# Making the second table's angles on ScalarE, turning the tables early, and putting y0 between the token halves

## The chip, the cores and the metric

The kernel runs on one core of one Trainium2 chip. The metric is the device time of one execution in microseconds (us), taken as the median of several runs; lower is better. In the notes, PE is the matmul engine, PEld its weight loads, DVE is VectorE, ACT is ScalarE, POOL is GpSimd and SP the engine that issues most stores.

## The reference

The input `x` is 8 sequences of 3008 tokens of 256 features. The reference takes the real part of a two-dimensional Fourier transform, and then a mixer over tokens and over channels:

```python
X = np.fft.fft(np.fft.fft(x, axis=1), axis=2).real          # x: 8 x 3008 x 256
h = np.maximum(X.transpose(0, 2, 1) @ w_tok1, 0.0) @ w_tok2  # 3008 -> 256 -> 3008
u = X + h.transpose(0, 2, 1)
out = u + np.maximum(u @ w_ch1, 0.0) @ w_ch2                 # 256 -> 1536 -> 256
```

The channel products at the end are most of the arithmetic. The kernel never forms the Fourier transform along the tokens in full: it splits the length 3008 into 64 times 47 and carries the second split's tables (`tp` and `tq`, cosine and sine of 2 pi k r / 3008) into `w_tok1`, which gives the "carried" weights `hp` and `hq`.

## The kernel before

Before any product can run, the tables have to be made on the chip: an angle is computed, brought into one period (`reduced`: multiply and add 2^23, take it off again, add), and put through ScalarE's Sin. For `tp` VectorE does the angle arithmetic, for `tq` GpSimd does it.

```python
def reduced(m, period, nrow, width, eng=nc.vector):
    v = gen.tile([P, width], FP32, tag="gv", bufs=2, name="gv")[0:nrow, :]
    eng.tensor_scalar(out=v, in0=m, scalar1=1.0 / period, scalar2=TWO23, op0=AT.mult, op1=AT.add)
    eng.tensor_scalar(out=v, in0=v, scalar1=-TWO23, scalar2=-float(period), op0=AT.add, op1=AT.mult)
    r = gen.tile([P, width], FP32, tag="gr", bufs=2, name="gr")[0:nrow, :]
    eng.tensor_tensor(out=r, in0=v, in1=m, op=AT.add)
    return r

def angles3(off, eng):
    m3 = gen.tile([P, 768], FP32, tag="m3", bufs=2, name="m3")
    ts(m3[:], kb[:], reff[:], AT.mult, off[:], AT.add, eng=eng)
    return reduced(m3[:], S, P, 768, eng)

table3(tp, angles3(offp, nc.vector))
# ... small tables on VectorE (ident, anti, md, t1n, t1b) ...
r3q = angles3(offq, pl)                # pl is GpSimd
```

Each batch then has a front: VectorE (batch 0) or GpSimd (later batches) folds the input (`fold`: xd, xp, eo), PE makes stage 1 (`pz`, copied to `z`) and stage 2 (`pw`, copied to `w`), and in batch 0 the carried weights (`ph`) in rounds between the `pw` products. The tail of the front is the token mixer: two halves of `w_tok1` products (`pt`), with `sq`, `uv` and `uu` made of them by ScalarE and VectorE; a small product `px` with a permutation that fills one column of `w`; thirds of `y` (`third`); and then the `w_tok2` products (`pu`).

```python
for th in range(2):
    c = slice(th * P, (th + 1) * P)
    pt = ps_f("pt1")                   # ps_f: a PSUM tile of 512 f32, three buffers in turn
    for o, n, f, hw in ((0, 130, 0, hp), (130, 127, 132, hq)):
        for g in range(NG):
            nc.tensor.matmul(pt[:, o:o + n], lhsT=hw[:, g, c], rhs=w[:, g, f:f + n], ...)
    if th == 0:
        px = ps_f("px")                # its own tile
        nc.tensor.matmul(px[:, 0:NG], lhsT=perm[:], rhs=w[:, :, 130], start=True, stop=True)
        nc.scalar.activation(out=w[:, :, 131], in_=px[:, 0:NG], func=AFT.Copy)
    sq = ...; nc.scalar.activation(out=sq[:], in_=pt[:, 130:257], func=AFT.Copy)
    # ... uv by VectorE from pt and sq, uu by ScalarE from uv ...
    yield
# ...
for c in range(NCH):
    if c < 3:
        third(c)
        yield
    # ... pu = w_tok2 products from uu; ut = pu + y ...
```

Every `yield` gives PE's turn back to the channel products of the previous batch, so one "step" of `w_ch1` products (`pc`, 6 products of 512 columns, about 1.3 us) and one of `w_ch2` products (`po`) stand between two pieces. At the front of batch 0 there is no previous batch, and short dummy products (`filler`) fill some gaps.

## Time and profile before

The kernel before takes 635.52 us in the rounds shared with the changed kernel. Its profiled execution has a span of 634.1 us. First the head of its profile page (span, busy time of each engine, and the clock granted to PE in 40 slices, in tenths):

```profile
span 634.1 us, 11971 instructions
PE 610.8 (96%) x4806; PEld 422.4 (67%) x4806; DVE 356.7 (56%) x807; ACT 315.8 (50%) x677; POOL 248.7 (39%) x238
PEclk9999999999999999999999999999999999999999
```

PE is busy 96% of the span, so only PE's idle time can be won. Where that idle time lies is shown by busy time in windows (columns: the window, its length, then busy us and instruction count of PE, PEld, DVE, ACT and POOL, PE's granted clock, DMA share, GB/s):

```profile
0.00:20.44 20.44, 6.47 (x47) 5.01 (x48) 18.37 (x55) 10.60 (x17) 18.52 (x30) 1.00 0.99 148
20.44:28.48 8.04, 6.51 (x66) 5.11 (x67) 6.50 (x15) 7.38 (x12) 6.99 (x16) 1.00 1.09 216
28.48:35.80 7.32, 7.07 (x73) 6.22 (x74) 5.43 (x16) 6.37 (x20) 1.93 (x2) 1.00 1.27 206
35.80:43.23 7.43, 6.12 (x87) 4.96 (x85) 3.63 (x12) 3.22 (x11) 0.00 (x0) 1.00 1.05 208
43.23:634.10 590.87, 584.65 (x4538) 401.12 (x4535) 322.80 (x712) 288.23 (x618) 221.30 (x191) 1.00 0.44 82
```

The windows are cut at events: first stage-1 product 20.44, first `pw` 28.48, first token product 35.80, first `w_ch1` product 43.23. From 43.23 us on PE is nearly always busy; this stretch is called the loop below. All of PE's other idle time is in the front, 0 to 43.23 us. The clock column reads 1.00 also where the trace holds no clock record, which is before 23.65 us here, so an early 1.00 says nothing: 16 fillers took 1.91 us from 21.22 us here.

What holds the front is VectorE. Here is VectorE's timeline just before and in the fold (start, us, engine, line, operation, out<-in, shapes, count):

```profile
13.00 0.81 DVE L87 TENSOR_SCALAR t1n<-cs,mask_149 94x48 f16<-94x48 f32 x1
13.72 0.23 DVE L87 TENSOR_SCALAR t1n<-cs,xicol 94x48 f16<-94x48 f32 x1
13.87 0.84 DVE L89 TENSOR_SCALAR t1b<-cs,xicol 94x24 f16<-94x24 f32 x1
14.71 0.68 DVE L393 TENSOR_TENSOR xd<-xp,xm 94x1024 f16<-94x1024 f16 x1
15.42 2.18 DVE L394 TENSOR_TENSOR xp<-xp,xm 94x1024 f16<-94x1024 f16 x1
...
24.75 0.48 DVE L402 TENSOR_TENSOR eo<-xd 94x635 f16<-94x635 f16 x1
```

and GpSimd's timeline beside it:

```profile
13.85 0.84 POOL L228 TENSOR_SCALAR gv<-gv 128x768 f32<-128x768 f32 x1
14.77 2.28 POOL L231 TENSOR_TENSOR gr<-gv,m_198 128x768 f32<-128x768 f32 x1
```

The same table operation takes 0.81 us once and 0.23 us the next time, and the fold's first xp add takes 2.18 us where all its like take about 0.7. The 0.84 us and the 2.18 us end within 0.6 us of the end of a GpSimd operation. The fold ends at 25.23 us.

### The profile page before, as it was taken

The page shows a single profiled execution, that of the slowest core. Times are in us where ns is not written, and L with a number is a line of the kernel's source. Part 1 is how long each engine was busy: PE and PEld are TensorE (multiplying, and loading weights), DVE is VectorE, ACT ScalarE, POOL GpSimd, SP SyncE. Part 2 cuts the span into 40 slices and gives each one's busy share as a digit, 9 for nine tenths or more (in the row PEclk, how much of TensorE's full clock was granted, in tenths as well). Part 3 has the DMA queues.
Part 4 walks back from the last instruction along what each step waited for, and adds up shares of the span by engine and source line. Part 5 has one row for each costly group of instructions (what it writes and reads, how often), then busy time and mean ns, then how long its engine had stood idle before and what let it go on. Part 6 is the DMA issues. An engine that isn't in the chain of part 4 may idle for free.

```text
span 634.1 us, 11971 instructions
## 1 busy us (share of the span) xinstructions
PE 610.8 (96%) x4806; PEld 422.4 (67%) x4806; DVE 356.7 (56%) x807; ACT 315.8 (50%) x677; POOL 248.7 (39%) x238
## 2 busy tenths in 40 slices
PE   2789999999999999999999999999999999999996
PEld 1665667667666776667667676666766676666664
DVE  8866545675764556545664547645565456644442
ACT  6667465654436553374435554365444644334441
POOL 8739789497030960259220790049300000000000
PEclk9999999999999999999999999999999999999999
DMA  8992662916613459152962249433222422323432
GB/s 133 210 173 84 127 126 42 161 46 119 130 34 67 101 101 103 45 98 51 141 95 62 57 85 119 83 75 84 51 51 63 88 52 51 83 67 83 60 84 66
DMA packets 86583, 56.28 MB, mean 89 GB/s; under 512 B 54864, under 2 KB 83472, under 8 KB 85776
## 3 DMA queue, kind: packets, MB, share of 16 engines
q1 hardware_dynamic: 78048, 37.84, 31.3%
q0 software_dynamic: 8256, 17.49, 16.6%
q8 instruction: 37, 0.61, 0.4%
q10 hardware_dynamic: 224, 0.20, 0.1%
q14 instruction: 18, 0.15, 0.1%
HBM read 34.98 MB, written 24.64 MB: 94 GB/s over the span
## 4 chain that ended last, share of the span: by engine, by line
PE 92%; issue 1%; ACT 1%; DVE 0%; DVEq 0%; ACTq 0%
PE po L566 39%; PE pc L545 38%; PE pu L512 6%; PE pz L415 1%; PE py L485 1%; PE pq L485 1%; PE pw L443 1%; PE pw L442 1%; PE pz L431 0%; PE pz L425 0%; ACT c_714 L548 0%; DVE osb L583 0%; PE pt_5989 L457 0%; PE pt_4067 L457 0%; PE pt_3176 L457 0%
## 5 line engine op out<-in xcount | busy, mean ns | idle before, releaser
L545 PE MATMUL pc<-ut,wc1p 128*128 128x512 f16 x576 | 140.2, 379 | 0.4 <-DVE ut L520 0.2
L545 PE MATMUL pc<-ut,wc1m 128*128 128x512 f16 (+1 forms) x576 | 134.9, 370 | 0.0
L583 DVE TENSOR_TENSOR osb<-po,rt 128x258 f32<-128x258 f32 (+4 forms) x246 | 75.2, 356 | 50.2 <-PE po L566 44.1
L545 PEld LDWEIGHTS <-wc1m 128*128 128x128 f16 x576 | 54.8, 98 | 53.8
L545 PEld LDWEIGHTS <-wc1p 128*128 128x128 f16 x576 | 52.9, 98 | 49.1 <-issue 2.1
L520 DVE TENSOR_TENSOR ut<-pu,yt 128x512 f16<-128x512 f32 (+1 forms) x96 | 64.4, 672 | 19.7 <-PE pu L512 19.7
L393 POOL TENSOR_TENSOR xd<-xp,xm 94x1024 f16<-94x1024 f16 x28 | 59.3, 2119 | 19.3 <-DMA xm<-in_x_dram,ix_76 19.3
L394 POOL TENSOR_TENSOR xp<-xp,xm 94x1024 f16<-94x1024 f16 x28 | 59.4, 2121 | 2.2
L398 POOL TENSOR_TENSOR eo<-xp 94x512 f16<-94x512 f16 (+1 forms) x28 | 34.0, 1213 | 59.1 <-PE pz L431 57.9
L276 ACT ACTIVATE z<-pz 128x480 f16<-128x480 f32 (+1 forms) x61 | 39.7, 668 | 27.1 <-PE pz L415 22.0
L512 PE MATMUL pu<-w2p,uu 128*128 128x512 f16 (+1 forms) x168 | 50.0, 379 | 0.0
L276 ACT ACTIVATE w<-pw 128x127 f16<-128x127 f32 x96 | 25.8, 280 | 47.0 <-PE pw L443 47.0
L490 DVE TENSOR_TENSOR yt<-py,qs 128x512 f16<-128x512 f32 x48 | 30.9, 686 | 30.9 <-PE pc L545 15.6
L445 DVE SCALAR_TENSOR_TENSOR w<-alt,pw 128x131 f16<-128x131 f16 x96 | 32.8, 351 | 18.6 <-ACT w L276 18.6
L603 POOL COPY ch<-c_7328 128x768 f16<-128x768 f16 x1 | 0.8, 825 | 84.5 <-DVE c_7328 L87 84.5
L402 POOL TENSOR_TENSOR eo<-xd 94x508 f16<-94x508 f16 (+1 forms) x28 | 33.7, 1204 | 0.0
L512 PEld LDWEIGHTS <-uu 128*128 128x128 f16 x192 | 18.7, 98 | 12.5 <-ACT sq L466 1.0
L488 ACT ACTIVATE qs<-pq 128x512 f32<-128x512 f32 x24 | 14.4, 601 | 19.3 <-PE pq L485 9.3
L442 PE MATMUL pw<-td_190,z 128*128 128x128 f16 x96 | 20.4, 220 | 0.9 <-DVE z L274 0.7
L415 PEld LDWEIGHTS <-eo 94*128 94x128 f16 x240 | 15.8, 101 | 7.9 <-DVE eo L400 2.5
L605 POOL COPY c_7994<-ch 128x768 f16<-128x768 f16 x1 | 0.8, 828 | 51.2 <-PE po L566 51.2
L415 PE MATMUL pz<-t1n,eo 94*128 94x96 f16 x240 | 18.6, 211 | 2.1 <-DVE eo L400 2.1
(429 smaller groups left out, 1169.4 us busy)
## 6 DMA issues: line engine op xcount, KB each, us to landing
out_dram<-osb SPq DMA_DIRECT2D x83, 256.0 KB, 3.6
xp<-in_x_dram POOLq DMA_DIRECT2D x16, 272.0 KB
out_dram<-osb SPq DMA_DIRECT2D x11, 192.0 KB, 3.0
xp<-in_x_dram POOLq DMA_DIRECT2D x16, 127.5 KB
rt<-ut SPq DMA_TRANSPOSE x96, 3.7
w2s<-in_moe_w_tok_dram POOLq DMA_DIRECT2D x1, 1504.0 KB
w1p<-in_moe_w_tok_dram POOLq DMA_DIRECT2D x2, 384.0 KB
wc_148<-in_moe_w_ch_dram POOLq DMA_DIRECT2D x1, 768.0 KB
```

What stands on the lines that cost most here:

```text
L276: nc.scalar.activation(out=out_, in_=in_, func=AFT.Copy)
L393: eng.tensor_tensor(out=xd[:, t, :], in0=xp[:, t, :], in1=rv, op=AT.subtract)
L394: eng.tensor_tensor(out=xp[:, t, :], in0=xp[:, t, :], in1=rv, op=AT.add)
L398: eng.tensor_tensor(out=eo[:, t, 1:129], in0=xp[:, t, 1:129], in1=xp[:, t, 255:127:-1], op=AT.add)
L402: eng.tensor_tensor(out=eo[:, t, 129:256], in0=xd[:, t, 1:128], in1=xd[:, t, 255:128:-1], op=AT.subtract)
L415: nc.tensor.matmul(pz[:, 96 * k:96 * k + 96], lhsT=eo[:, t0 + k, c], rhs=t1n[:].rearrange("p a b k -> p (a b k)"), start=True, stop=True)
L445: nc.vector.scalar_tensor_tensor(out=w[:, g, 0:131], in0=alt[:], scalar=pw[:, 131:132], in1=pw[:, 0:131], op0=AT.mult, op1=AT.add)
L512: nc.tensor.matmul(pu[:, 0:n], lhsT=uu[:, th, int(minus), h, :], rhs=w2_cols(b, c)[:, th], start=(th == 0), stop=(th == 1))
L520: nc.vector.tensor_tensor(out=ut[:, h, f0:f0 + n].rearrange("p (a b) -> p a b", b=64), in0=pu[:, 0:n].rearrange("p (b a) -> p a b", b=64), ...
L545: nc.tensor.matmul(pc[:, 0:n], lhsT=wc[:, h, ct * P:(ct + 1) * P], rhs=ut[:, h, f0:f0 + n], start=(h == 0), stop=(h == 1))
L566: nc.tensor.matmul(po[0:n, o:o + D], lhsT=c1[:, ct, ks * P:ks * P + n], rhs=wc2[:, ct, :], start=(ct == 0), stop=(ct == NCT - 1))
L583: nc.vector.tensor_tensor(out=osb[r, ks_, j], in0=src[r, k0:k1, j], in1=rt[r, ks_, p], op=AT.add)
```

## The change

The intent was to free the front of batch 0. The angles of `tq` leave GpSimd, where they held VectorE (0.81 us for 0.23 and 2.18 us for about 0.7, above): three ScalarE passes with Identity and one VectorE operation make them. The second table is turned before stage 1. Two of the twelve `w_tok1` (carried) products go before the end of the fold, and the rounds shrink from seven to six. The `px` product moves ahead of the token products, into a free corner of the products' own PSUM tile, which saves a tile and a late copy. `y`'s first third (y0) goes between the two token halves. The core of the diff:

```diff
-    table3(tp, angles3(offp, nc.vector))
+    for o, i, scale, bias in ((mq, kb, reff[:], offq), (vq, mq, 1.0 / S, up),
+                              (vq, vq, 1.0, down)):
+        nc.scalar.activation(out=o[:], in_=i[:], func=AFT.Identity, scale=scale, bias=bias[:])
+    ts(mp[:], kb[:], reff[:], AT.mult, offp[:], AT.add)
+    table3(tp, reduced(mp[:], S, P, 768))
...
-    r3q = angles3(offq, pl)
+    nc.vector.scalar_tensor_tensor(out=vq[:], in0=vq[:], scalar=-float(S), in1=mq[:],
+                                   op0=AT.mult, op1=AT.add)
...
-        for th in range(2):
+        def tok1(th):
             pt = ps_f("pt1")
+            if th == 0:
+                nc.tensor.matmul(pt[:, 260:260 + NG], lhsT=perm[:], rhs=w[:, :, 130], ...)
+                nc.scalar.activation(out=w[:, :, 131], in_=pt[:, 260:260 + NG], func=AFT.Copy)
             for o, n, f, hw in (...):          # the token products into pt
-            if th == 0:
-                px = ps_f("px")                # px product and its copy, cut
...
+        tok1(0)
+        yield
+        third(0)
+        yield
+        tok1(1)
+        yield
...
     turn(tp, tts_p, 8)
-    turn_rows(tts_p, 1.0, 24)
+    table3(tq, vq)
+    turn_rows(tts_p, 1.0, 0)
     take(fold(0, [nc.vector] * 4), 4)
+    turn(tq, tts_q, 4)
     own = front(0)
     take(own, 2)
-    filler(16)
-    table3(tq, r3q)                            # ... turn(tq), turn_rows between stage-1 parts, cut
+    turn_rows(tts_q, -1.0, 16)
     take(own, 2)
-    for g2 in range(NG // 2 + 1):
-        if g2 < NG // 2:
-            take(own, 2)
-            carried(tts_p, hp, g2, 0)
-        if g2 > 0:
-            carried(tts_q, hq, g2 - 1, g2 % 3 > 0)
+    for g2 in range(2):
+        carried(tts_p, hp, g2, 0)
+    take(own, 4)
+    for g2 in range(NG // 2):
+        take(own, 2)
+        if g2 < 4:
+            carried(tts_p, hp, g2 + 2, 0)
+        carried(tts_q, hq, g2, g2 < 4)
```

More of the change, by code (lines that the diff above doesn't have):

```diff
@@ L293 @@
     sin(cs[0:KR, :], r1, PI2 / 47)
-    def angles3(off, eng):
-        m3 = gen.tile([P, 768], FP32, tag="m3", bufs=2, name="m3")
-        ts(m3[:], kb[:], reff[:], AT.mult, off[:], AT.add, eng=eng)
-        return reduced(m3[:], S, P, 768, eng)
-    table3(tp, angles3(offp, nc.vector))
+    up, down = pvec("up"), pvec("down")
+    nc.vector.memset(up[:], TWO23)
+    nc.vector.memset(down[:], -TWO23)
+    mp, mq, vq = (gen.tile([P, 768], FP32, tag=n, name=n) for n in ("mp", "mq", "vq"))
+    for o, i, scale, bias in ((mq, kb, reff[:], offq), (vq, mq, 1.0 / S, up),
+                              (vq, vq, 1.0, down)):
+        nc.scalar.activation(out=o[:], in_=i[:], func=AFT.Identity, scale=scale,
+                             bias=bias[:])
+    ts(mp[:], kb[:], reff[:], AT.mult, offp[:], AT.add)
+    table3(tp, reduced(mp[:], S, P, 768))
     ident = const.tile([P, P], FP16, tag="ident")
@@ L451, in front @@
         uu = perb.tile([P, 2, 2, 2, P], FP16, tag="uu", name="uu", bufs=2)
-        for th in range(2):
+        def tok1(th):
             c = slice(th * P, (th + 1) * P)
             pt = ps_f("pt1")
+            if th == 0:
+                nc.tensor.matmul(pt[:, 260:260 + NG], lhsT=perm[:], rhs=w[:, :, 130],
+                                 start=True, stop=True)
+                nc.scalar.activation(out=w[:, :, 131], in_=pt[:, 260:260 + NG],
+                                     func=AFT.Copy)
             for o, n, f, hw in ((0, 130, 0, hp), (130, 127, 132, hq)):
@@ L459, in front @@
                                      start=(g == 0), stop=(g == NG - 1))
-            if th == 0:
-                px = ps_f("px")
-                nc.tensor.matmul(px[:, 0:NG], lhsT=perm[:], rhs=w[:, :, 130],
-                                 start=True, stop=True)
-                nc.scalar.activation(out=w[:, :, 131], in_=px[:, 0:NG], func=AFT.Copy)
             sq = perb.tile([P, 127], FP32, tag="sq", name="sq", bufs=2)
@@ L476, in front @@
                 nc.scalar.activation(out=o, in_=i, func=AFT.Relu)
-            yield
         yt = perb.tile([P, 2, HALF], FP16, tag="yt", name="yt")
@@ L502, in front @@
         for c in range(NCH):
-            if c < 3:
+            if c in (1, 2):
                 third(c)
@@ L612 @@
     turn(tp, tts_p, 8)
-    turn_rows(tts_p, 1.0, 24)
+    table3(tq, vq)
+    turn_rows(tts_p, 1.0, 0)
     take(fold(0, [nc.vector] * 4), 4)
+    turn(tq, tts_q, 4)
     own = front(0)
     take(own, 2)
-    filler(16)
-    table3(tq, r3q)
+    turn_rows(tts_q, -1.0, 16)
     take(own, 2)
-    turn(tq, tts_q, 0)
-    take(own, 2)
-    turn_rows(tts_q, -1.0, 0)
-    take(own, 2)
-    for g2 in range(NG // 2 + 1):
-        if g2 < NG // 2:
-            take(own, 2)
-            carried(tts_p, hp, g2, 0)
-        if g2 > 0:
-            carried(tts_q, hq, g2 - 1, g2 % 3 > 0)
+    for g2 in range(2):
[6 more added lines that the diff above has]
+        carried(tts_q, hq, g2, g2 < 4)
     take(own, 5)
```

## The prediction

> **What bounds the kernel now.** The page shows PE busy 610.8 of 634.1 us (96%); the chain of waits is 92% PE. Busy time by windows: from the first w_ch1 product (43.23 us) to the end PE is busy 584.65 of 590.87 us, over 4 us of the rest being the last output write. Only the front, 0 to 43.23 us, can give anything; PE idles 17 us there. 2% (12.7 us) is out of reach.
>
> **The front's chain (timelines of the engines).** VectorE tables to 14.7, VectorE fold 14.71 to 25.23, stage-1 z copies to 28.4, pw/ph rounds 28.48 to 35.8 (about 1.13 us each), token tail 35.8 to 43.23.
>
> **What the change does.**
> 1. GpSimd loses four 768-wide operations (11.69 to 17.05 us). Meanwhile VectorE was held: small table operations took 0.81 and 0.84 us where a like one took 0.23, the fold's first xp add 2.18 where the next took 0.71; each ended just after a GpSimd operation.[...] Weight-load issues take their place, beside which two-input VectorE work ran undisturbed at 18.4 to 20 us. I count 2.5 to 3 us back.
> 2. VectorE gains one 768-wide scalar_tensor_tensor (0.96 us, as the like-sized add). Net: fold starts near 14.4 without the 1.5 us hold and ends near 23.5 instead of 25.2.
> 3. ScalarE gains three 768-wide Identity passes (0.85 us each, from Sin passes of that width) in its idle 6.2 to 8.64 us: tp's Sin moves 0.1 us.
> 4. tq's Sin, transposes and row turns go ahead of stage 1; two of twelve w_tok1 products start before the fold ends. PE runs half-speed there (0.107 us per 128 columns before 23.5 us)[...]. First pw product: 26.4 to 27.2 instead of 28.48.
> 5. Rounds: 6.6 us to the last pw and its VectorE copy, against 7.3; but the perm product now comes first and waits for that copy.
> 6. Tail: VectorE does yt (1.29 us) before the second uv, so the second half's uu comes about 1.3 us later; yt no longer stands before ut. With the 24 fillers (1.4 us) still ahead of the first w_ch1 product: about 8.0 us against 7.43, which takes back most of 5.
> 7. Steady state: same matmuls. Only one w_ch1 step (1.3 us) now stands between the second half and its first w_tok2 product, whose operand is ready after about 1.5 us: 0 to 0.1 us loss per batch.
>
> **Sum.** First pw 1.3 to 2.1 us earlier, rounds and tail about even, 0.3 us of early main-loop gaps saved, up to 0.6 us lost later: 635.1 less 1.7 is **633.4 us** (median). 80% range **631.6 to 635.3**. Chances: faster by over 2% 0.01, within 2% 0.98, slower 0.01.
>
> **What would show it.** (1) fold's first xp add 0.7 us, small table operations 0.23, fold end near 23.5. (3) no new wait before tp's Sin. (4) first pw before 27.3. (6) PE idle before the first pu; first w_ch1 product near 41.5. (7) later batches 72 to 74 us each, as before.
>
> **What would make it wrong.** w_tok1 landing later than about 23 us (estimated from bytes moved), so early products stall PE in order; PE slow into the rounds; weight-load issues holding VectorE[...] (total then nil); a larger wait in later batches.

## More of the kernel before

The experiments were made on three chips, called A, B and C here; the runs of one group share their own runs of the kernel before. On which chip the first comparison of the two kernels ran is not recorded.

In a later batch, PE's timeline shows the token products with the small `px` product after them:

```profile
148.54 1.47 PE L566 MATMUL po<-wc_148,c_1860 128*128 128x256 f16 x12
149.85 0.85 PE L457 MATMUL pt_2137<-w,hp 128*128 128x130 f16 x12
150.54 0.84 PE L457 MATMUL pt_2137<-w,hq 128*128 128x127 f16 x12
151.21 0.18 PE L462 MATMUL px<-w,perm 128*128 128x12 f16 x1
151.24 1.46 PE L545 MATMUL pc<-ut,wc1p 128*128 128x512 f16 x6
```

Nothing waits: each group starts where the one before it ends (the recorded durations of neighbouring groups overlap by 0.15 to 0.17 us here).

## The result

The changed kernel takes 639.82 us (638.92 to 640.9, four runs) against 635.52 us (635.12 to 636.81, four runs). The ratio is 1.0065, with a 95% interval of 1.0041 to 1.0089. A ratio here is the mean time of one kernel's runs over that of the other kernel's in the same rounds, so it is not quite the ratio of the medians quoted. The interval lies above 1: the change costs about 4 us. The predicted 633.4 us, and the whole predicted range up to 635.3 us, missed it.

The head of the profile page after:

```profile
span 638.7 us, 11923 instructions
PE 610.8 (96%) x4786; PEld 420.1 (66%) x4786; DVE 353.9 (55%) x810; ACT 320.1 (50%) x680; POOL 244.2 (38%) x234
PEclk9799999999999999999999999999999999999999
```

PE's busy sum is unchanged, although 20 fillers are gone; the clock row has a 7 in the second slice. The same windows as before, cut at the same events (the third starts at the first `pw` and ends at the first token product, which is now the `px` product):

```profile
0.00:17.18 17.18, 5.09 (x40) 3.39 (x40) 15.12 (x58) 15.17 (x23) 14.64 (x27) 1.00 0.90 137
17.18:26.65 9.47, 5.22 (x62) 3.81 (x63) 6.68 (x15) 6.45 (x12) 6.68 (x15) 0.91 1.24 213
26.65:35.84 9.19, 8.50 (x65) 6.90 (x65) 6.04 (x16) 5.99 (x18) 1.93 (x2) 0.73 1.21 206
35.84:44.51 8.67, 6.08 (x86) 4.95 (x86) 3.67 (x11) 3.11 (x11) 0.65 (x1) 1.00 0.96 190
44.51:638.70 594.19, 585.95 (x4539) 401.06 (x4536) 322.38 (x711) 289.37 (x618) 220.28 (x191) 1.00 0.43 81
```

The first `pw` comes 1.83 us earlier (26.65 against 28.48), the rounds take 1.87 us more (9.19 against 7.32, at a mean clock of 0.73), the token tail takes 1.24 us more (8.67 against 7.43), and the loop takes 3.32 us more (594.19 against 590.87). That is the whole difference of 4.6 us between the spans.

VectorE's timeline, the lines that answer to those above:

```profile
11.56 0.24 DVE L87 TENSOR_SCALAR t1n<-cs,mask_149 94x48 f16<-94x48 f32 x1
...
11.87 0.33 DVE L89 TENSOR_SCALAR t1b<-cs,xicol 94x24 f16<-94x24 f32 x1
...
12.10 0.95 DVE L335 SCALAR_TENSOR_TENSOR vq<-vq,mq 128x768 f32<-128x768 f32 x1
12.96 0.68 DVE L399 TENSOR_TENSOR xd<-xp,xm 94x1024 f16<-94x1024 f16 x1
13.68 0.69 DVE L400 TENSOR_TENSOR xp<-xp,xm 94x1024 f16<-94x1024 f16 x1
...
21.68 0.48 DVE L408 TENSOR_TENSOR eo<-xd 94x635 f16<-94x635 f16 x1
```

The holds are gone (0.24 for 0.81, 0.33 for 0.84, 0.69 for 2.18), and the fold ends at 22.16 us, 3.07 us earlier. The intended part of the change works, and better than predicted (the fold was to end near 23.5).

What PE did with it (PE's timeline, with the idle time before an instruction and what ended it in brackets):

```profile
19.54 0.63 PE L421 MATMUL pz<-t1n,eo 94*128 94x96 f16 x10
20.99 0.28 PE L369 MATMUL ph<-w1p,tt 128*128 128x256 f16 x1 [0.82 <-DMA w1p<-in_moe_w_tok_dram]
23.23 0.27 PE L371 MATMUL ph<-w1m,tt 128*128 128x256 f16 x1 [1.96 <-DMA w1m<-in_moe_w_tok_dram]
...
23.99 0.59 PE L421 MATMUL pz<-t1n,eo 94*128 94x96 f16 x10
...
26.65 0.29 PE L448 MATMUL pw<-td_199,z 128*128 128x128 f16 x1 [0.68 <-DVE z L274]
```

The early carried products stop PE until `w_tok1` has landed, 2.78 us in two waits (0.82 and 1.96). The last stage-1 products come behind them in PE's order, so they start at 23.99 us although their input was ready at 22.16. PE's windows just after that (same columns, PE only):

```profile
27.00:28.00 1.00, 1.00 (x8) 0.50 1.05 218
33.00:34.00 1.00, 1.00 (x14) 1.00 1.43 196
```

In a window of 1 us PE is fully busy both times, but does 8 instructions at clock 0.50 and 14 at clock 1.00. Rounds that take 1.13 us in the kernel before take 2.14 us here.

And PE's timeline in a later batch:

```profile
224.78 1.47 PE L579 MATMUL po<-wc_148,c_2838 128*128 128x256 f16 x12
226.09 0.18 PE L463 MATMUL pt_3088<-w,perm 128*128 128x12 f16 x1
226.60 0.85 PE L469 MATMUL pt_3088<-w,hp 128*128 128x130 f16 x12 [0.32 <-ACT w L465]
227.28 0.84 PE L469 MATMUL pt_3088<-w,hq 128*128 128x127 f16 x12
...
236.27 0.66 PE L525 MATMUL pu<-w2p,uu 128*128 128x512 f16 x2
```

The `px` product and the token products now write one PSUM tile, and the first token product waits for ScalarE's copy out of it: 0.51 us from the start of one to the start of the other, in every batch. The list of PE's waits in the loop has this line for seven batches; the one before has no such line. From the third batch on, a batch takes 0.53 to 0.55 us longer (start of `px` to start of `px`: 74.97, 73.66, 74.98 us where before it took 74.43, 73.12, 74.43).

### The profile page after: what moved, and what is told of

Same layout as the page of the kernel before. It is cut to its first block, busy times and chain, and to the rows that moved or that the text cites. A ratio compares the mean times of both kernels' runs of the same rounds, so it can differ in the third digit from the quotient of the medians.

```text
span 638.7 us, 11923 instructions
## 1 busy us (share of the span) xinstructions
PE 610.8 (96%) x4786; PEld 420.1 (66%) x4786; DVE 353.9 (55%) x810; ACT 320.1 (50%) x680; POOL 244.2 (38%) x234
## 4 chain that ended last, share of the span: by engine, by line
PE 94%; DMA 2%; DVE 2%; ACT 1%; POOL 1%; issue 0%; DVEq 0%; POOLq 0%
PE po L579 39%; PE pc L558 38%; PE pu L525 7%; DMA w1m<-in_moe_w_tok_dram 2%; PE pz L421 1%; PE pw L448 1%; PE pw L449 1%; PE py L492 1%; PE pq L492 1%; PE ph L371 0%; PE ph L369 0%; POOL xm L118 0%; PE pz L437 0%; PE pz L431 0%; ACT w L465 0%
## 5 line engine op out<-in xcount | busy, mean ns | idle before, releaser
L449 PE MATMUL pw<-td_198,z 128*128 128x131 f16 x96 | 20.9, 228 | 0.0
L118 POOL DMA_INDIRECT xm<-in_x_dram,ix_76 x16 | 15.8, 990 | 11.1 <-DMA w2s<-in_moe_w_tok_dram 6.1
```

## The experiments

Three costs were suspected: the `px` product in the products' tile (the tile); the stop on the early products with the slow clock behind it (the clock); and the new order, where only one step is left between the second token half and the first `w_tok2` product (the order). They are rivals for where the loss lies; a further rival was that the gain in the fold is worth nothing on PE. Later, theory L says that the issue of a gather on GpSimd makes a ScalarE copy late and that the new order exposes it, and rival R that the new order has a fixed loss. All seventeen runs gave correct results. The table gives medians, the ratio to the kernel before in the same rounds, and from the profiled run the first `pw`, the first `w_ch1` product and the length of the loop (from that product to the end).

| run | chip | us | ratio (95%) | first pw | first w_ch1 | loop |
|---|---|---|---|---|---|---|
| before | | 635.52 | | 28.48 | 43.23 | 590.9 |
| after | | 639.82 | 1.0065 (1.0041 to 1.0089) | 26.65 | 44.51 | 594.2 |
| e1_px_own | A | 638.77 | 1.0050 (1.0036 to 1.0064) | 26.27 | 42.86 | 594.1 |
| e2_late | A | 639.87 | 1.0070 (1.0057 to 1.0083) | 24.71 | 41.06 | 595.4 |
| e3_fill | A | 641.06 | 1.0081 (1.0064 to 1.0098) | 26.07 | 41.56 | 595.8 |
| e4_order | A | 638.81 | 1.0055 (1.0036 to 1.0073) | 25.66 | 41.94 | 594.0 |
| e5_px_order | B | 634.29 | 0.9969 (0.9956 to 0.9983) | 26.43 | 42.19 | 590.6 |
| e6_front_warm | B | 632.54 | 0.9951 (0.9937 to 0.9964) | 25.27 | 39.90 | 590.7 |
| e7_tail_only | B | 643.09 | 1.0114 (1.0098 to 1.0129) | 27.86 | 44.31 | 595.4 |
| e8_angles_only | B | 632.79 | 0.9955 (0.9941 to 0.9970) | 25.04 | 39.77 | 590.6 |
| e9_load_later | C | 635.40 | 0.9995 (0.9970 to 1.0020) | 26.35 | 42.92 | 590.9 |
| e10_split_z | C | 635.37 | 0.9998 (0.9964 to 1.0032) | 24.92 | 39.55 | 590.6 |
| e11_late_px_order | C | 633.29 | 0.9960 (0.9948 to 0.9973) | 24.69 | 40.93 | 590.6 |
| e12_fill_px_order | C | 634.78 | 0.9979 (0.9965 to 0.9993) | 26.00 | 41.78 | 590.6 |
| e13_px_own_again | C | 634.53 | 0.9989 (0.9970 to 1.0009) | 26.21 | 41.22 | 590.9 |
| e14_load_moved | C | 635.33 | 0.9997 (0.9984 to 1.0011) | 25.87 | 42.49 | 590.8 |
| e15_moved_order | C | 634.18 | 0.9973 (0.9960 to 0.9986) | 25.93 | 41.74 | 590.6 |
| e16_px_own_third | C | 636.65 | 0.9999 (0.9985 to 1.0013) | 27.54 | 44.42 | 590.9 |
| e17_load_moved_again | C | 635.44 | 0.9982 (0.9964 to 1.0000) | 26.67 | 43.29 | 590.9 |

Two readings help. The loop separates a cost per batch from a cost in the front. And the loop has a floor near 590.6 us: every run with the old order and the own tile has 590.6 or 590.7, and the kernel before 590.9.

### e1_px_own: the perm product in its own PSUM tile

```diff
             if th == 0:
-                nc.tensor.matmul(pt[:, 260:260 + NG], lhsT=perm[:], rhs=w[:, :, 130], ...)
-                nc.scalar.activation(out=w[:, :, 131], in_=pt[:, 260:260 + NG], func=AFT.Copy)
+                px = ps_f("px")
+                nc.tensor.matmul(px[:, 0:NG], lhsT=perm[:], rhs=w[:, :, 130], ...)
+                nc.scalar.activation(out=w[:, :, 131], in_=px[:, 0:NG], func=AFT.Copy)
```

> The changed kernel with one edit: the perm product gets a PSUM tile of its own again (still ahead of the token products). Theory P[...]: the 0.45 us PE stop between the perm product and the first token product goes in all eight batches, so about 3.2 to 3.6 us less than the changed kernel (near 636.3 us), and the stretch from the first w_ch1 product to the end falls from 594.2 to about 591. Rival (the wait is for w, whose column 131 ScalarE writes, whatever the PSUM tile): the stop stays and the time with it (639.8). Second rival (what costs later is y0 between the halves): also unchanged.

The wait is gone from every batch: the first token product starts at 223.52, 0.03 us after the `px` product at 223.49. But the loop was still 594.1 us, and the time fell by about 1 us only (ratios 1.0065 and 1.0050, whose intervals overlap). A new line stood in the list of PE's waits in the loop, 2.9 us in three batches, for ScalarE's `uu`:

```profile
PE pu L525 <- ACT uu L483: 2.9, 3, 1.1
```

There the copy `sq` of the second half had started 1.04 to 1.25 us late. So the tile explains the wait, and on this chip it is not all of the loss.

### e2_late, e3_fill: the early products

e2 put the early products back into the rounds of the kernel before (the seven-round loop of the diff). e3 kept them and put `filler(36)` ahead of them, to keep PE busy while `w_tok1` lands.

```diff
# e2
-    for g2 in range(2):
-        carried(tts_p, hp, g2, 0)
     take(own, 4)
-    for g2 in range(NG // 2):                  # six rounds, p two rounds ahead of q
+    for g2 in range(NG // 2 + 1):              # seven rounds, p one round ahead of q, as before
# e3
+    filler(36)
     for g2 in range(2):
         carried(tts_p, hp, g2, 0)
```

> The changed kernel with one edit: the two early w_tok1 products go back into the rounds, loop as in the kernel before. Theory D (the early products wait for the second w_tok1 load, and with that keep the last stage-1 slices and the whole front waiting): first pw near 25.0 instead of 26.65, no wait for the w_tok1 load, and if PE also keeps full speed the first w_ch1 product comes about 3 us earlier (41.5), total near 636.8. If only the clock matters [...]rounds stay at half speed and the gain is 1 us or less.

> The changed kernel with one edit: 36 fillers (about 2 us) ahead of the early products, inside the wait for the w_tok1 load. Theory C (the idle PE lost its clock): the wait for the load still ends near 23.2 and the first pw stays near 26.6, but the granted clock stays 1.00, the first three rounds take 1.1 us each instead of 2.15, and the time falls by 2.5 to 3 us (near 637). Rival (the rounds are slow for another reason, such as DMA traffic): granted clock or round times unchanged, no gain.

Both profiles show a full clock through the rounds (the means of the two profiled runs are 0.998 and 0.999), and with it the time from the first `pw` to the `px` product was 6.81 us in e3, where after has 9.19 and I had predicted 6.6. So the slow clock is what the rounds lost, about 2.4 us in that profile. But both kernels were no faster than after in the median: their loops were 595.4 and 595.8 us, with the tile's stop in every batch and three late `sq` copies each (0.39 to 0.72 us). The clock explains the rounds, and the front is the smaller part of the loss.

### e4_order: y0 behind both halves

```diff
         tok1(0)
         yield
-        third(0)
-        yield
         tok1(1)
         yield
+        third(0)
+        yield
```

> The changed kernel with one edit: both token halves ahead of y0, as in the kernel before. My count says y0 between the halves costs about 0.6 us in the first batch's tail and 0.07 us in each of seven later ones (the first w_tok2 product waits for uu): 0.6 to 1.2 us less than the changed kernel (near 638.8). Rival (y0 between is a gain, as the change intended): slower than 639.8 by some tenths. If it were the main cause of the loss: 3 us or more less.

The list of PE's waits in e4's loop (engine, line, what for: us in total, times, longest us):

```profile
PE pt L469 <- ACT w L465: 2.3, 7, 0.3
```

This is the tile's stop alone, and no wait for `uu`. The loop is 594.0 us: 3.4 us above the floor, with the order of the kernel before. One second-half copy was 0.33 us late here too, and it cost nothing, because two more steps stand behind it.

### e5_px_order: both mended

The edit is that of e1 and that of e4 together.

> The changed kernel with the perm product in its own PSUM tile and both token halves ahead of y0. Own tile alone took the 0.45 us stop away, yet three batches then lost 1.1 us each: ScalarE's copy of the second half's products began about 0.9 us late and the first w_tok2 product, now only one w_ch1 step behind, waited for it. Theory S (y0 between the halves takes the slack that hid this): with the old order the stretch from the first w_ch1 product to the end is that of the kernel before, 590.9 within 0.5, and the time is about 634 to 635.5. Rival (the loop loss has a further cause): the stretch stays at 594.

The loop falls to 590.6 us, and the kernel is faster than before: 634.29 us, 0.9969. Each mend alone had brought about 1 us, no more than the intervals allow for, and both together bring about 6 us (by the ratios, 1.0065 less 0.9969, as the runs were on different chips). The two are not independent: e1 left the late copies exposed, and e4 left the tile's stop.

### e7_tail_only, e8_angles_only: the parts alone on the kernel before

e7 is the kernel before with only the new token part (px first in the same tile, y0 between the halves). e8 is the kernel before with only the ScalarE angles.

```diff
# e7, on the kernel before
-        for th in range(2):                    # with px in its own tile, after the products
+        def tok1(th):                          # with px in pt, ahead of the products
...
+        tok1(0); yield; third(0); yield; tok1(1); yield
...
-            if c < 3:
+            if c in (1, 2):
# e8, on the kernel before
-    r3q = angles3(offq, pl)
+    # three Identity passes on ScalarE and one operation on VectorE, as in the change
...
-    table3(tq, r3q)
+    table3(tq, vq)                             # still in its old place
```

> The kernel before with only the change's token part: perm product first and in the products' PSUM tile, y0 between the halves. If this part alone makes the loop loss: 0.5 us more in each batch, the stretch after the first w_ch1 product 594 instead of 590.9, the first w_ch1 product about 0.5 to 1 us later, total 639 to 640. Rival (loss comes from the new front): 635 to 636.

> The kernel before with only ScalarE's angles for the second table (GpSimd's four operations gone). Fold ends near 22.2 instead of 25.2 as in the changed kernel. If the chain behind the fold follows it: first pw about 2 to 3 us earlier, total about 632.5 to 633.5. Rival (second table's turns and z copies then hold the rounds, or the clock is lost): gain under 1 us.

The token part alone costs 0.0114 (about 7.2 us against the 635.94 us of the same rounds), the angles alone bring 0.0045 (2.9 us of 635.94). The sum of the ratios, +0.0069, is close to the whole change's +0.0065, so the early tables and products come to about nothing net. That is an estimate: e7's profile has three late `sq` copies (0.32 to 0.34 us, described under e9) that the profile of after has not. e8's fold ends at 22.14 us, as early as in the whole change, and its clock is full from 16.78 us to the last product: the gain comes from taking GpSimd's angle operations away. This also disposes of the rival: a faster fold is worth about 3 us on PE.

### e6_front_warm: a version meant to win

e6 has the angles and the early tables, the rounds and the token part of before, and 32 and 10 fillers around the last stage-1 products. Its front differs from the changed kernel's in this (cut):

```diff
-    for g2 in range(2):
-        carried(tts_p, hp, g2, 0)
+    filler(32)
     take(own, 4)
+    filler(10)
     # seven rounds as in e2; the token part of the kernel before
```

> The change's angles and early table turns alone, with the w_tok1 products back in the rounds, the token tail of the kernel before, and 42 more fillers where PE would idle before the rounds. If the fold's 3 us can be carried through: first pw near 24.8, rounds at 1.13 us, first w_ch1 product near 39.5 to 40, the rest 590.9; total 631.5 to 632.5, faster than both kernels. Rival (the front is pinned by something later, such as the weights or the second batch's input): the rest grows by what the front saved, total about 635.

It takes 632.54 us, 0.9951, and beats both kernels, but it does not beat e8 (0.9955) by anything that the intervals could tell. The early tables need not be paid for.

### e9_load_later: a run that tested nothing

> The changed kernel with the perm product in its own PSUM tile (as before: 638.8 us, three batches losing 1.1 us each to a copy of the second half's products that ScalarE began 0.9 to 1.2 us late), and one more edit: each loop's fold and next input load are issued two steps later. In the earlier run every late copy fell within 1.2 us of the end of the load's second gather on GpSimd. Theory L (the late copy goes with that load): with the load moved away no copy is late, the stretch after the first w_ch1 product falls from 594.1 to about 591.4, time about 635.5 to 636. Rival (the late copies belong to the place in the program, not to the load): same three batches late, 638 to 639.

Theory L came from this: in the profiles of before and of the runs on chips A and B, in the batches after the first, the second half's copies that were over 0.3 us late were exactly those where the half's last product ended between 0.63 us before and 0.36 us after the end of the issue of the next input's second gather on GpSimd. That was 17 of 17, and none of the others was late. (In the profile of after, three ended 0.38 and 0.39 us after it and were not late.) e9 was to move the load by asking for it at 12 instead of 8 pieces:

```diff
-                if done >= 8 and not folded:
+                if done >= 12 and not folded:
```

It came out at 635.4 us with no late copy and a loop of 590.9 us, which looks like a proof of L. It is none. Comparing the orders of the two built programs afterwards showed e9's instructions to be the same as e1's on every engine: in GpSimd's order the load stands behind the same fold in both. e9 was e1 on another chip. In both profiles the half's products end 0.11 to 0.15 us before the gather in three batches; on chip A the copies were late, on chip C not.

### e10_split_z

e10 is e6 with one of the two z copies of a stage-1 pair moved from VectorE to ScalarE.

```diff
-                copy(b == 0 and t0 == 1, zo[:, :, :, t0:t0 + 5], ...)
+                copy(b == 0 and t0 == 1 and half == 0, zo[:, :, :, t0:t0 + 5], ...)
```

> An attempt at a still better version: the warm-front kernel (632.5 us) with the z copies of the last five slices split between VectorE and ScalarE (ScalarE idle 1.2 us there) instead of both on VectorE. First pw at about 24.8 instead of 25.3, time 0.4 us less; a null result if the rounds then wait on ScalarE.

Its runs fell into two groups, 632.2 to 633.0 us and 637.7 to 638.5 us, so the ratio of 0.9998 (0.9964 to 1.0032) says nothing about the z copies. It is inconclusive. The mean granted clock is 1.000 in the three faster runs and 0.994 to 0.995 in the three slower ones, so the clock may have a part in it. But that is about 7 us at half clock, which can cost 3.5 us at most (estimates from these means), and the groups are over 5 us apart.

### e11_late_px_order, e12_fill_px_order: the early products on the mended kernel

e11 is e5 with the early products put back (e2's edit), e12 is e5 with 36 fillers ahead of them (e3's edit).

> The changed kernel with own PSUM tile and old half order (634.3 us) and also the two early w_tok1 products back in the rounds. If the early products are a loss (they wait for the load in order, and PE loses its clock): first pw 24.7 to 25.2 instead of 26.4, full clock, 632.3 to 633 us. Rival (they use time that would be lost anyway): 634.3 or more.

> The same kernel (634.3 us) with the early products kept and 36 fillers ahead of them. Separates the wait from the clock: granted clock 1.00 through the rounds, rounds from first to last pw 5.8 us instead of 7.3, first pw still near 26.2; 632.7 to 633 us. If the clock cost nothing: 634.3.

With the loop at its floor, the early products are worth -0.1% at most: 0.9960 without them, 0.9969 with them (e5, on chip B), 0.9979 with them and fillers, and the intervals overlap. That matches the "about nothing" of e7 and e8. Both profiles were again at half clock for about 3.4 us (from 26 us in e11, from 27 us in e12), although e11 has no wait for `w_tok1` at all, and e12 only one of 0.32 us. So the stop on `w_tok1` is not needed for the clock to fall, and the fillers did not prevent it here. That the wait for `w_tok1` by itself causes the half clock, as I had thought, did not hold up.

### e13 and e16 (e1 again, twice), e14 and e17 (the load really moved), e15 (that with the old order)

e13 and e16 are e1, byte for byte. e14 and e17 are e1 with the next input's load behind the last copy of the batch, and this time GpSimd's order was checked to differ. e15 is e14 with the old order of y0.

```diff
-                    if b + 3 < BB:
-                        x_tiles[b + 3] = load_x(b + 3)
             if c + 1 == NCH:
                 pair(b, c1)
+                if b + 3 < BB:
+                    x_tiles[b + 3] = load_x(b + 3)
```

> Byte for byte the kernel of the own-tile run (638.77 us, ratio 1.005, on one chip), whose engine streams the void load run (635.4 us, ratio 0.9995, on another chip) shared. It is the control for the two runs beside it on this chip. If late ScalarE copies come and go by the run (theory L, with its size set by when the gather's issue ends): between 634 and 639 us, and its profile shows 0 to 3 second-half copies over 0.3 us late, each of them ending within about 0.6 us of the end of an input gather's issue on GpSimd. If the place where the cost sits is the order alone (rival R, a fixed loss of the new order): 638 to 639 us again on any chip.

> The same kernel with the next input's load issued at the end of the batch, after the 64-column copy, so that GpSimd is doing the load some 25 us after the second half's products and not beside them; this time GpSimd's own order of instructions is changed, which was checked before. Theory L (the gather's issue makes ScalarE's copy late and the new order exposes it): no late copy at all in the later batches, the loop 590.5 to 591.2 us, 633.5 to 635 us, and faster than the control by whatever late copies the control shows (0 to 4 us). Rival R (a fixed loss of the order, which has nothing to do with the gather): the same time as the control, within 1 us, and late copies still there. If the load now comes too late for the fold, PE will wait in stage 1 (pz from eo), which would add time in every batch and show as such.

> The moved load together with the old order (y0 after both halves). The old order had cost nothing with late copies, so theory L and rival R differ in the step from the run before: L says the same time as the moved load with the new order, within 0.7 us; R says 3 to 4 us faster than it. Both expect 633.5 to 635 us here if the moved load does no harm elsewhere.

> The own-tile kernel a third time, wanted on another chip than the last two jobs. In the last job (the chip of the void load run) the second half's products ended 0.10 to 0.13 us before the gather's issue in three batches, as they had in the first own-tile run, and ScalarE's copies were prompt there; the first run's were 1.04 to 1.25 us late. If late copies go with the chip: late copies and 637 to 640 us on a chip like the first, none and 634 to 635.5 us on one like the last. If they go by chance from run to run on any chip, the five rounds will show both times here.

> The moved load again, beside the own-tile kernel on the same chip. If the chip shows late copies in the own-tile kernel, theory L says this one has none and takes 634.5 to 636 us, 2 to 4 us less; rival R (the order costs this much by itself) says both take the same. If the own-tile kernel shows no late copies here either, the pair again tells nothing, and it stays open what made them.

All five fell on chip C. No second-half copy was late in any of them, in e13 and e16 with three of them ending 0.10 to 0.15 us before the gather. So there was nothing for the moved load to remove, and e14 and e17 tell nothing about the gather. What the five do tell is that rival R, a fixed loss of the new order, is wrong: with the own tile the loop is 590.9 us with the new order (e13, e16) and 590.6 with the old (e15, against 590.8 in e14, which differs from it in the order alone), 0.3 us for the whole loop. The 3.3 us of e1 on chip A appeared with the late copies and not without them. One kernel's time differs between chips and jobs: 638.77 us on chip A (e1), 634.53 and 636.65 us in two jobs on chip C (e13, e16).

How the late copy looks. First ScalarE's copy in e1 on chip A, and the `w_tok2` product that waits for what is made of it:

```profile
307.50 0.28 ACT L473 ACTIVATE sq<-pt 128x127 f32<-128x127 f32 x1 [3.40 <-PE pc L558]
```

```profile
308.87 0.39 PE L525 MATMUL pu<-w2p,uu 128*128 128x512 f16 x1 [0.90 <-ACT uu L483]
```

The half's last product ended at 306.46 (it started at 305.62 and took 0.84 us), so this copy starts 1.04 us late. The bracket names a later `pc` product as the releaser, which is an inference of the profile. In e13 on chip C the same copy has the token product itself as its releaser and starts 0.04 us after it (303.60):

```profile
303.64 0.28 ACT L473 ACTIVATE sq<-pt 128x127 f32<-128x127 f32 x1 [2.39 <-PE pt L469]
```

e13 and e16 together give the cleanest measure of the clock, since they are one kernel on one chip with equal loops. PE's wait for the second part of `w_tok1` and two windows of the rounds, in e13:

```profile
22.83 0.27 PE L371 MATMUL ph<-w1m,tt 128*128 128x256 f16 x1 [1.25 <-DMA w1m<-in_moe_w_tok_dram]
```

```profile
26.00:28.00 2.00, 1.79 (x21) 1.00 1.01 207
28.00:30.00 2.00, 2.00 (x25) 1.00 1.07 210
```

and in e16:

```profile
23.77 0.27 PE L371 MATMUL ph<-w1m,tt 128*128 128x256 f16 x1 [2.04 <-DMA w1m<-in_moe_w_tok_dram]
```

```profile
26.00:28.00 2.00, 0.91 (x8) 0.50 1.05 219
28.00:30.00 2.00, 2.00 (x14) 0.50 1.03 202
```

In these rounds e13 keeps the full clock and reaches the first `w_ch1` product at 41.22 us; e16 loses it and gets there at 44.42. That is the whole difference of their spans (632.1 and 635.3). Of the 3.2 us, 1.33 are in the first `pw` (26.21 and 27.54: the later load, and stage 1 already partly slow) and the rest in the rounds.

Over all profiles, of the fourteen with the early tables and without e6's fillers, eleven ran at half clock for some us between about 25 and 32 us, and three (e2, e3, e13) did not. The profiles of the five others (before, e6, e7, e8, e10) did not. (e13, e14, e16 and e17 also ran at half clock for 3.4 us between 16.8 and 21.3 us, in stage 1.) Most of the eleven had waited 1.15 to 2.04 us for `w_tok1`, but e13 waited 1.25 and kept its clock, and e11 and e12 lost it with no or little wait (PE's longest idle just before the fall was 1.03 us in e11). The size is better settled than the trigger. Taking the clock in the windows from 24 to 32 us as a mix of 0.50 and 1.00, the time spent at half clock comes to 3.40 us in e1 and e5, 3.42 in e12, 3.44 in e4 and e17, and 6.82 in after and in e16. So it comes in one unit of 3.4 us or in two, and the two that lost two units are those with the longest waits for `w_tok1` (1.96 and 2.04 us).

What goes ahead of it shows when the profiles are cut at the clock records' own steps of 3.41 us, up to 45 us. In the step just before each of the fifteen falls to half clock PE was busy for 40 to 60% of the time: 1.60 of 3.41 us in after (from 21.45 us), 1.37 in e16 (from 21.26). None of the 76 steps at full clock with PE busy for 61% or more was followed by a fall. But 14 steps with 48 to 60% were not either: 2.04 of 3.41 us in e13 (from 24.28) kept the clock that 2.06 in e17 (from 24.19) lost. So a PE idle for some 40% of a step went with every fall, and was not enough for one; what else decides stays open.

In the profiles the half clock in the rounds goes with the new front, but a profile is one run. The mean clocks say that the kernel before loses its clock too: of its 45 runs beside the experiments, 31 have a mean of 0.990 to 0.996, where the four runs of after have 0.993 to 0.997 (half clock after the last product, up to 2.6 us in the profiles, accounts for 0.002 at most). Only the profiled run's windows are kept, so where before lost it is not known. It cost little there: runs of before at 1.000 span 633.5 to 634.1 us, those at 0.990 to 0.992 span 634.7 to 635.2. That the profile of before has a full clock is in part luck, and how much of the change's median loss is the clock is not shown.

## Why the prediction was wrong

The predicted span is 634.1 less 1.7, or 632.4 us; the measured one is 638.7. Of the 6.3 us, 3.0 are in the front (first `w_ch1` product near 41.5, measured 44.51) and 3.3 in the loop (590.9, measured 594.2).

- **Items 1 to 3 were right, and their gain undersized.** With GpSimd's angle operations gone, the first xp add fell from 2.18 to 0.69 us and the small table operations fell too (0.81 to 0.24, 0.84 to 0.33). That VectorE ran slower beside these operations is measured; why it did is not shown, and the reason that item 1 gave is cut. ScalarE's three passes took 1.01, 0.94 and 0.94 us, for the 0.85 that item 3 estimated. The fold ended at 22.16 against the predicted 23.5. The "1.5 us hold" was the first xp add; the small tables and the fold's start gained more than I counted. The weight-load issues that took their place did not hold VectorE (0.68 and 0.69 us for the first xd and xp, beside an issue from 12.62 to 14.55 us). e8 confirms it alone: 0.45% faster.
- **Item 4 was right in its number:** first `pw` 26.65, predicted 26.4 to 27.2. But it is right for two errors that cancel: the fold was 1.3 us earlier than thought, and the wait on `w_tok1`, which I had named as a risk and not counted, took it back. e8, without early products, has its first `pw` at 25.04.
- **Item 5 failed: "Rounds: 6.6 us to the last pw and its VectorE copy".** Measured 9.19 us. PE turned fast 9 us earlier than in the kernel before (the first clock record, at 1.00, starts at 14.62 us, against 23.65), and then fell back to half clock (0.50) at 24.9 us and stayed there for 6.8 us, two units of 3.4 us. "PE slow into the rounds" is among the risks at the end of the prediction, but losing a full clock again is in none of its items. That one kernel can lose its clock in one run and keep it in another is shown in the rounds of e16 and e13 (0.50 and 1.00 from 26 to 30 us). With a full clock the rounds take 6.81 us (e3, e13), so by that comparison 2.4 us of the 2.6 missed are this.
- **Item 6 was undersized:** "about 8.0 us against 7.43", measured 8.67. From the `px` product to the first `w_ch1` product it takes 8.20 us with px in its own tile (34.66 to 42.86 in e1, 33.02 to 41.22 in e13), so y0's new place cost about what I had said, and the remaining 0.47 us are the tile's stop in batch 0.
- **Item 7 failed, and is the largest: "Steady state: same matmuls ... 0 to 0.1 us loss per batch".** Its part on the order was right where no copy is late: the wait is 0.07 us (the first pair of `pu` products takes 0.66 us where it took 0.59). What I had not seen is that the moved `px` product shares a PSUM tile with the products behind it, and that PE then waits for ScalarE's copy, although the columns differ (260 to 271 against 0 to 256): 0.51 us from one product to the other, in each batch, against 0.03 us with two tiles (e1). The diff's line `pt[:, 260:260 + NG]` was there to be read. e4 shows this cost alone (loop 594.0), and e5 shows it gone (590.6). In the profile of after, where no copy is late, seven stops of 0.48 us each (0.51 less the 0.03 of e1) make 3.4 us, an estimate that covers the loop's whole 3.3.
- **A second cost of item 7's order comes and goes.** On chips A and B, ScalarE's copy of the second half was late in three batches (e1, e2, e3, e7), and the new order has no slack for it: up to 3.3 us in e1. On chip C it did not appear, with the same engine streams and the same neighbours in time (e9, e13, e16), nor in the profile of after. Shown is that it is the slack that decides whether a late copy costs: e6, with the old order, had a copy 1.14 us late and a loop of 590.7 us, where each of e1's three (1.04 to 1.25 us late) cost 1.0 to 1.2 us. What makes the copy late is open. The end of the gather's issue was near each late copy, but is not enough to make one, and the run that would settle it (the moved load on a chip with late copies) was not had.

## What to carry to other kernels

When a small product is moved ahead of a large one, look at which PSUM tile it writes: a copy out of a tile that the next products write puts the other engine's latency into PE's order (0.51 us from product to product here), and once per batch that can outweigh the gain in the front (3.4 us here, against about 3). Where PE takes its instructions in order, a product placed early "because it is free" can stop all behind it on a load (2.78 us in two waits here), so give it a place only if its operands are known to have landed. When a change has several parts, run each alone: the angles alone (632.79 us) were the better change, and the parts that seemed free cost more than it had gained.
